# A fused attention and MLP kernel: the opening of token block 0 split by contraction chunk, gelu kept in PSUM, and block 1's input loaded later

## The chip, the cores and the metric

The kernel runs on one core of a Trainium2 chip. The metric is the device time of one execution in microseconds (us); lower is better. A measurement of this kernel is the median of several executions.

## The reference, cut to what matters

```python
xn = layernorm(x)                                  # x: 2048 tokens x 640
qkv = xn @ wqkv                                    # 32 heads of 20
phi(z) = concat(softmax(z @ w_phi[h]), softmax(-(z @ w_phi[h])))
A = (phi(q) @ (phi(k)^T v)) / (phi(q) @ sum(phi(k)) + 1e-6) @ wo
y = layernorm(xn)
B = gelu(y @ w1 + b1) @ w2 + b2                    # 640 -> 1728 -> 640
out = x + A + B
```

Everything is float32. The kernel splits each operand into a high and a low float32r part and makes a product of three matmuls (high times high, high times low, low times high).

## The kernel before, in words

The 2048 tokens are four blocks of 512. The results are kept transposed, as five chunks of 128 features by 512 tokens (`acc[b]`, which begins as the block's transposed x). The hidden layer of the MLP has 14 chunks of 128, taken two at a time (g = 0 to 6). For one pair and one block, a **pass** (`passes`) makes two hidden chunks, each of 15 matmuls of 128x512 with y as the right side (L70, L71 and L72, in `mm3`), then gelu on ScalarE (L286), a split of its result into `hh` and `hl` (copy on ScalarE at L61, subtraction on VectorE at L64), and then five output tiles of six matmuls each with the hidden pair as the right side. VectorE adds each output tile to `acc[b]` (L329 for g = 0, L331 later), and this frees the tile's PSUM bank. Output tiles take banks 5, 6, 7 in turn (`self.po`), so the fourth tile of a row of tiles waits until the first has been added. Hidden chunks take banks 0, 1, 2 (`self.ph`).

**The opening** is written out by hand: TensorE, VectorE, ScalarE and GpSimd run their instructions in the order of the code there. Block 0 is prepared from x itself. Four tiles of 128 tokens are loaded (`xb`); VectorE takes their means and variances (L138, L139); ScalarE subtracts the mean (L166, `centre`); each tile is multiplied by its factor `ry` (`scale`: even tiles on VectorE at L172, odd ones on ScalarE at L170); TensorE transposes the 128x128 pieces (L181, `make_y0`), and ScalarE and VectorE split the transposed pieces into the high and low part of `y[0]`. This is done for two tiles (256 tokens) at a time. After each half come 30 matmuls of 128x256 (L549, `half_first`): they make that half of the hidden chunks 0 and 1. Their results are turned into hidden values later by the list `zs`. Before the first transposes, 18 matmuls on zeros (L579) run.

**Block 1** is prepared otherwise: its means and factors are turned into rows by one small transpose (L197, `rows`), written to DRAM from ScalarE's DMA queue (L202), and read back as one broadcast of 128 x 1024 values (L207, `m<-r`). From `acc[1]` (all of x transposed, loaded at L512), GpSimd subtracts the row of means, chunk by chunk (L677); VectorE multiplies by the row of factors (L679), ScalarE makes the high part (L681) and VectorE the low part (L683). These steps are spread over the matmuls of block 0 by the generator `next_y`: one step of it runs at each `tick`, which is once for three matmuls.

DMAs of the main queue are issued by SyncE, in an order that a scheduler chooses; `issue_after` holds a DMA behind another in that order. The other lines that the text names: L63 copies weights on VectorE, L193 gathers the means for the rows, L199 takes the transposed rows out of PSUM, L646 multiplies attention weights, L669 subtracts in the attention weights `wpt`, L775 to L803 prepare blocks 2 and 3 in the same way later.

```python
p00 = mlp.passes(0, 0, [wc[0], wc[1]], hid)     # output tiles of block 0, hidden chunks 0 and 1
mlp.beside = next_y()
p10 = mlp.passes(1, 0, [wc[2], wc[3]])          # hidden chunks 2 and 3 of block 0
next(p10)                                       # its two hidden chunks
finish(p00)                                     # five output tiles
for m, _ in enumerate(p10): ...                 # five more
```

After these, block 1 begins with the hidden chunks 0 and 1.

Of the kernel before, what the change touches and what calls it, by code (L numbers as in the profile page):

```python
# [8 lines left out]
F32 = mybir.dt.float32  # L9
F32R = mybir.dt.float32r  # L10
AF = mybir.ActivationFunctionType
ALU = mybir.AluOpType
# [39 lines left out]
def tile_kernel(ctx: ExitStack, tc: tile.TileContext, x, xT, wkT, wqT, wv, wphi, wo, w1, b1, w2, b2,  # L52
                ident, mmask, emask, vsel, out):
    nc = tc.nc
# [43 lines left out]
    acc = [None] * NB  # L98
# [69 lines left out]
    def scale(t, xb, act=False):  # L168
        if act:
            nc.scalar.activation(xb, xb, AF.Copy, scale=ry[:, t:t + 1])  # L170
        else:
            nc.vector.tensor_scalar_mul(xb, xb, ry[:, t:t + 1])  # L172

    def make_y0(half, xbs, ptile):

        cols = slice(half * 256, half * 256 + 256)
        for c0, n in ((0, 2), (2, 2), (4, 1)):
            ps = ptile()
            for c in range(n):
                for i in range(2):  # L180
                    nc.tensor.transpose(ps[:, c * 256 + i * P:c * 256 + (i + 1) * P],  # L181
                                        xbs[i][:, (c0 + c) * P:(c0 + c + 1) * P], idt)
            src = ps[:, :n * 256].rearrange("p (c t) -> p c t", c=n)
            cs = slice(c0, c0 + n)
            split(y[0][0][:, cs, cols], y[0][1][:, cs, cols], src)
            yield

    def rows(b, n, xp, ptile, wait, queue=nc.sync):

        sc = xp.tile([P, n, 2, 4], F32, name="sc", bufs=1)  # L190
        ts = slice(4 * b, 4 * b + 4 * n)
        for a, src in enumerate((mv[:, ts, 0], ry[:, ts])):
            nc.vector.tensor_copy(sc[:, :, a, :], src.rearrange("p (b t) -> p b t", b=n))  # L193
        for _ in range(wait):
# [7 lines left out]
        queue.dma_start(r_dram[n].rearrange("b r t -> (b r) t"), sr)  # L202
# [8 lines left out]
    loads = {}  # L211


    class Mlp:
# [67 lines left out]
        def gelu(self, g, j, pz, gt, hh, hl, out=False):  # L282
            if out:
                nc.vector.tensor_copy(gt, pz)
                pz = gt
            nc.scalar.activation(gt, pz, AF.Gelu_apprx_tanh, bias=b1t[:, 2 * g + j:2 * g + j + 1])  # L286
            split(hh, hl, gt)

        def passes(self, g, b, ws, hid=None):


            yh, yl = y[b]
            self.turn ^= 1
            todo = ()
            if hid is None:
                hid, todo, gts = [], ws, mtile(4)
            for j, (w1h, w1l, w2h, w2l) in enumerate(todo):
                gt = gts[:, j, :512]
                hs = mtile(self.hid[self.turn][j], F32R)
                hh, hl = hs[:, 0, :512], hs[:, 1, :512]  # L300
                if not (g == 6 and j == 1):
                    self.first(g, j, b, ws[j], gt, hh, hl)
                    hid.append((hh, hl))
                else:
                    pz = self.ph()
                    for kc in range(KC):
                        nc.tensor.matmul(pz, w1h[:, kc, :], yh[:, kc, :], start=kc == 0, stop=False)
                        nc.tensor.matmul(pz, w1l[:, kc, :], yl[:, kc, :], start=False, stop=kc == KC - 1)
                    tm = gt[0:64, :]
                    nc.scalar.activation(tm, pz[64:128, :], AF.Copy)  # L310
                    nc.vector.tensor_tensor(tm, pz[0:64, :], tm, op=ALU.add)
                    nc.scalar.activation(gt[0:64, :], tm, AF.Gelu_apprx_tanh, bias=b1t[0:64, 13:14])
                    nc.scalar.activation(hh[0:64, :], gt[0:64, :], AF.Copy)
                    nc.gpsimd.tensor_tensor(hh[64:128, :], gt[0:64, :], f(hh[0:64, :]), op=ALU.subtract)
                    hid.append((hh, None))
            yield
            for m in range(KC):
                pw = self.po()
                ms = slice(m * P, (m + 1) * P)
                for j, (hh, hl) in enumerate(hid):  # L320
                    w2h, w2l = ws[j][2:]
                    if hl is not None:
                        mm3(pw, w2h[:, ms], w2l[:, ms], hh, hl, j == 0, j == 1)
                        self.tick()
                    else:
                        nc.tensor.matmul(pw, w2h[:, ms], hh, start=False, stop=False)  # L326
                        nc.tensor.matmul(pw, w2l[:, ms], hh, start=False, stop=True)  # L327
                if g == 0:
                    nc.vector.scalar_tensor_tensor(acc[b][:, m, :], pw, b2t[:, m:m + 1], acc[b][:, m, :], op0=ALU.add, op1=ALU.add)  # L329
                else:  # L330
                    nc.vector.tensor_tensor(acc[b][:, m, :], pw, acc[b][:, m, :], op=ALU.add)  # L331
                yield
# [178 lines left out]
    def load_acc(b):  # L511
        nc.sync.dma_start(acc[b], xT[:, b * 512:(b + 1) * 512].rearrange("(c p) t -> p c t", p=P))  # L512
# [4 lines left out]
    mlp = Mlp((0, 1, 2, 3), ((0, 2), (1, 3)))  # L517
# [19 lines left out]
    gts = mtile(4)  # L537
# [4 lines left out]
    def half_first(half, *order):  # L542

        cols = slice(half * 256, half * 256 + 256)
        pz = [pall()[:, cols] for _ in range(2)]
        last = {op[0]: op for op in order}
        for j, wi, yi in order:
            for kc in range(KC):
                nc.tensor.matmul(pz[j], wc[j][wi][:, kc, :], y[0][yi][:, kc, cols],  # L549
                                 start=(wi, yi, kc) == (0, 0, 0), stop=kc == KC - 1 and last[j] == (j, wi, yi))  # L550
        return [lambda j=j: mlp.gelu(0, j, pz[j], *[m[:, cols] for m in (gts[:, j, :512], *hid[j])]) for j in range(2)]

    x1 = load_x(range(4, 8), xp)
    for c, pool in ((2, None), (3, r0)):
# [27 lines left out]
    centre(0, x0[0])  # L582
    step(s01, 3)
    centre(1, x0[1])
    scale(0, x0[0])
    scale(1, x0[1], True)
    parts[0][0]()
    step(s23, 2)
    y01, y23 = make_y0(0, x0[:2], pall), make_y0(1, x0[2:], pall)
# [3 lines left out]
    step(s23, 1)  # L593
    centre(2, x0[2])
    centre(3, x0[3])
    scale(2, x0[2])
    scale(3, x0[3], True)
    zs = half_first(0, *((j, wi, yi) for j in range(2) for wi, yi in ((0, 0), (1 - j, j), (j, 1 - j))))
    parts[2][0]()
    step(s47, 2)  # L600
    step(y23, 4)
    zs += half_first(1, *((j, wi, yi) for ops in (((0, 0), (1, 0)), ((0, 1),)) for j in range(2) for wi, yi in ops))
    parts[3][0]()
    step(s47, 2)
    step(s01, 1)
    step(s47, 1)
    step(s47, 1)
    rows1 = rows(1, 1, xp, Banks(3), 1, nc.scalar)
    next(rows1)
    for c in range(2):  # L610
        parts[c][1](nc.vector)
# [41 lines left out]
    def next_y():  # L653

        for _ in range(3):
            yield
        next(rows1)
        for z in zs[:2]:
            z()
        finish(rows1)  # L660
        mr = load_rows(1)
        first_raws.extend(raws(jobs[0]))
        for z in zs[2:]:
            z()
        for c in range(2, 4):
            parts[c][1]()
        for _ in range(4):
            yield
        nc.vector.tensor_tensor(wpt[:, :, :, 1:], wpt[:, :, :, 1:], wpt[:, :, :, 0:1].to_broadcast([G6, 6, 6, DF]), op=ALU.subtract)  # L669
        for _ in range(9):  # L670
            yield
        xcs = {}
        for n in range(2 * KC + 5):
            c, i = divmod(n, 2)
            if i == 0 and c < KC:
                xcs[c] = xp.tile([P, D], F32, name="xb")[:, :512]
                nc.gpsimd.tensor_tensor(xcs[c], acc[1][:, c], mr[:, 0], op=ALU.subtract)  # L677
            if i == 0 and 0 <= (d := c - 1) < KC:
                nc.vector.tensor_tensor(xcs[d], xcs[d], mr[:, 1], op=ALU.mult)  # L679
            if i == 1 and 0 <= (d := c - 1) < KC:  # L680
                nc.scalar.activation(y[1][0][:, d], xcs[d], AF.Copy)  # L681
            if i == 0 and 0 <= (d := c - 2) < KC:
                nc.vector.tensor_tensor(y[1][1][:, d], xcs[d], f(y[1][0][:, d]), op=ALU.subtract)  # L683
            yield
        for st in (s23, s47):
            step(st, 1)
            yield
# [924 lines left out]
```

## Time and profile before

| | |
|---|---|
| median of 3 runs | 708.85 us (708.53 to 711.32) |
| the profiled execution | 709.98 us |
| its span, first to last instruction | 708.2 us |
| TensorE (PE) busy | 700.9 us, 99% of the span |
| VectorE (DVE) busy | 526.1 us, 74% |
| GpSimd (POOL) busy | 439.2 us, 62% |
| ScalarE (ACT) busy | 352.7 us, 50% |
| granted TensorE clock | 1.0 |

PEld is TensorE's loading of weights, which runs ahead of the matmuls. A row of the timeline has the start, the time taken, the engine, the line, the operation, what it writes and reads, the shape, how many instructions are merged in it, and in brackets the idle time of the engine before it and what ended that. A row of the waits has who waited for whom, the total in us, how often, and the longest. A row of the groups has the busy time and the mean in ns.

### The profile page before, as it was taken

How to read it: one execution, taken by the hardware profiler on the slowest of the kernel's cores; microseconds unless marked ns; L12 is line 12 of the kernel's file. 1: busy time of each engine (PE TensorE's matmuls, PEld its weight loads, DVE VectorE, ACT ScalarE, POOL GpSimd, SP SyncE). 2: the span in 40 equal slices, each digit the busy share in tenths (PEclk: the TensorE clock that was granted, in tenths of full speed). 3: DMA queues.
4: the chain of work that ended last, by engine and by line, in shares of the span. 5: the costliest groups of instructions: out<-in, count | busy, mean ns of one | idle time of the engine just before them, and what ended most of it. 6: DMA issues, size and time to landing. Idle time of an engine off the chain costs nothing.

```text
span 708.2 us, 9785 instructions
## 1 busy us (share of the span) xinstructions
PE 700.9 (99%) x3369; PEld 589.1 (83%) x3369; DVE 526.1 (74%) x840; ACT 352.7 (50%) x583; POOL 439.2 (62%) x374
## 2 busy tenths in 40 slices
PE   8999999999999999999999999999999999999998
PEld 7788888878888888888888888878888888888886
DVE  7877755978754788788888877838688686786773
ACT  6534554444433544554544546457676667561250
POOL 3621314567245998798787969558689997552530
PEclk9999999999999999999999999999999999999999
DMA  9823643475622227325500707874355659537212
GB/s 322 284 83 114 189 123 98 156 252 175 219 97 93 75 94 221 96 88 195 128 0 4 188 0 292 238 228 120 115 152 161 179 154 304 204 124 272 81 60 104
DMA packets 66296, 107.61 MB, mean 152 GB/s; under 512 B 7479, under 2 KB 31831, under 8 KB 64367
## 3 DMA queue, kind: packets, MB, share of 16 engines
q1 hardware_dynamic: 65942, 106.98, 47.5%
q8 instruction: 26, 0.43, 0.2%
q14 instruction: 24, 0.19, 0.1%
q10 hardware_dynamic: 304, 0.01, 0.0%
HBM read 72.42 MB, written 34.55 MB: 151 GB/s over the span
## 4 chain that ended last, share of the span: by engine, by line
PE 86%; DVE 5%; DMA 2%; issue 2%; POOL 2%; ACT 2%; SPq 1%; ACTq 0%; POOLq 0%; DVEq 0%
PE bank L906 28%; PE bank L70 16%; PE bank L71 16%; PE bank L72 16%; PE bank L976 3%; PE bank L646 2%; PE bank L1214 1%; PE bank L1215 1%; DMA t<-t 1%; DMA xb<-in_x 1%; DMA xq<-in_xT 1%; POOL w L64 1%; DVE st L138 1%; PE bank L327 1%; PE bank L326 1%
## 5 line engine op out<-in xcount | busy, mean ns | idle before, releaser
L906 PE MATMUL bank<-wkh,y 128*128 128x512 f32 (+1 forms) x480 | 139.5, 364 | 0.0
L64 POOL TENSOR_TENSOR w<-r,w 128x640 fp32r<-128x640 f32 x32 | 52.2, 1647 | 93.2 <-ACT w L61 63.4
L70 PE MATMUL bank<-m,w 128*128 128x512 f32 x274 | 108.1, 394 | 1.6 <-DVE acc L329 1.0
L71 PE MATMUL bank<-m,w 128*128 128x512 f32 x274 | 106.7, 389 | 0.0
L70 PE MATMUL bank<-y,w 128*128 128x512 f32 (+1 forms) x274 | 106.5, 389 | 0.0
L71 PE MATMUL bank<-y,w 128*128 128x512 f32 (+1 forms) x274 | 106.0, 387 | 0.0
L72 PE MATMUL bank<-y,w 128*128 128x512 f32 (+1 forms) x270 | 104.3, 386 | 0.0
L72 PE MATMUL bank<-m,w 128*128 128x512 f32 x262 | 102.0, 389 | 0.0
L906 PEld LDWEIGHTS bank<-wkh,y 128*128 128x128 f32 x480 | 87.5, 188 | 13.3
L906 PE MATMUL bank<-wkl,y 128*128 128x512 f32 (+1 forms) x240 | 87.4, 364 | 0.0
L942 ACT ACTIVATE m<-m,rs_all 128x1280 f32<-128x1280 f32 x32 | 43.7, 1365 | 42.9 <-POOL m L941 42.8
L70 PEld LDWEIGHTS bank<-m,w 128*128 128x128 f32 x274 | 51.5, 188 | 13.7 <-DVE acc L331 1.6
L70 PEld LDWEIGHTS bank<-y,w 128*128 128x128 f32 x274 | 51.5, 188 | 10.8 <-issue 0.4
L71 PEld LDWEIGHTS bank<-y,w 128*128 128x128 f32 x274 | 51.5, 188 | 10.5 <-DMA y<-t 0.3
L71 PEld LDWEIGHTS bank<-m,w 128*128 128x128 f32 x274 | 51.5, 188 | 10.2
L72 PEld LDWEIGHTS bank<-y,w 128*128 128x128 f32 x270 | 50.7, 188 | 10.3
L944 DVE TENSOR_REDUCE sm<-m 128x64 f32<-128x1280 f32 x32 | 47.4, 1482 | 15.0 <-ACT m L942 14.8
L72 PEld LDWEIGHTS bank<-m,w 128*128 128x128 f32 x262 | 49.2, 188 | 10.4
L906 PE MATMUL bank<-w,y 128*128 128x512 f32 x240 | 57.4, 391 | 0.0
L941 POOL TENSOR_TENSOR m<-m,mx 128x640 f32<-128x640 f32 (+2 forms) x48 | 44.4, 938 | 19.3 <-DVE mx L930 19.3
L331 DVE TENSOR_TENSOR acc<-bank,acc 128x512 f32<-128x512 f32 x70 | 46.9, 684 | 10.5 <-PE bank L72 5.3
L64 DVE TENSOR_TENSOR m<-m,m 128x512 fp32r<-128x512 f32 (+1 forms) x34 | 28.8, 854 | 34.4 <-ACT m L61 34.4
(216 smaller groups left out, 1517.2 us busy)
## 6 DMA issues: line engine op xcount, KB each, us to landing
r<-in_w SPq DMA_DIRECT2D x52, 320.0 KB
e<-e SPq DMA_DIRECT2D x40, 256.0 KB
e<-acc SPq DMA_DIRECT2D x52, 160.0 KB
acc<-in_xT SPq DMA_DIRECT2D x4, 1280.0 KB
t<-t SPq DMA_DIRECT2D x8, 512.0 KB
tf<-t SPq DMA_DIRECT2D x2, 1536.0 KB
xb<-in_x SPq DMA_DIRECT2D x8, 320.0 KB
t<-in_x SPq DMA_DIRECT2D x8, 320.0 KB
```

What stands on the lines that cost most here:

```text
L64: eng.tensor_tensor(lo, src, f(hi), op=ALU.subtract)
L70: nc.tensor.matmul(ps, lh, rh, start=first, stop=False, **kw)
L71: nc.tensor.matmul(ps, lh, rl, start=False, stop=False, **kw)
L72: nc.tensor.matmul(ps, ll, rh, start=False, stop=last, **kw)
L138: nc.vector.bn_stats(st[:, i, h, :], xb[:, h * 320:(h + 1) * 320])
L331: nc.vector.tensor_tensor(acc[b][:, m, :], pw, acc[b][:, m, :], op=ALU.add)
L646: nc.tensor.matmul(ps[:, u * nh * DF:(u + 1) * nh * DF], raw[:nh * DH, u * P:(u + 1) * P], wpt[:nh * DH, g, :nh, 1:], start=True, stop=True)
L906: nc.tensor.matmul(ps, lh[:, kc, c], rh[:, kc], start=n == 0, stop=n == 3 * KC - 1)
L941: subs[n, t] = nc.gpsimd.tensor_tensor(ep[:, s], a, b, op=ALU.subtract)
L942: exps[n, t] = nc.scalar.activation(e, e, AF.Exp, scale=rs_all[:, t:t + 1])
L944: nc.vector.tensor_reduce(sm, e.rearrange("p s (h f) -> p (s h) f", f=DH), axis=AX, op=ALU.add)
L976: nc.tensor.matmul(kvp[g // 2][:, (g % 2) * 240:(g % 2) * 240 + 240].rearrange("p (s f) -> p s f", s=4), v[:, g * VS:(g + 1) * VS], ft[:, ...
```

## The change

It has five parts.

1. In `make_y0` the transposed pieces come as one chunk, two chunks, two chunks (before: two, two, one). The odd tile of each pair is scaled in two pieces: the first 384 features on ScalarE and the last 256 on VectorE.
2. In the second half of block 0, the 20 matmuls that use the high part of y are ordered by contraction chunk (kc), over both hidden chunks and both parts of the weights. The ten with the low part follow. The first half keeps its order.
3. For blocks 0 and 1, gelu writes back into the PSUM bank that it reads, and the split reads that bank (before: an SBUF tile `gt`).
4. Block 1's `acc[1]` is not loaded with the early DMAs but behind `m<-r`, in two DMAs of two and three chunks. The row of means goes through a corner of `acc[1]`, and its transpose uses bank 7.
5. The row's DMA is issued after the first of the four half gelus instead of the second. The split of w2's chunk 2 has its copy on VectorE. The subtraction in `wpt` comes before the splits of the hidden chunks 2 and 3, and the split of w2's chunk 3 comes later.

```diff
+    def scale_pair(t):
+        scale(t, x0[t])
+        scale(t + 1, x0[t + 1][:, :3 * P], True)
+        scale(t + 1, x0[t + 1][:, 3 * P:])
     def make_y0(half, xbs, ptile):
-        for c0, n in ((0, 2), (2, 2), (4, 1)):
+        for c0, n in ((0, 1), (1, 2), (3, 2)):
     def rows(b, n, xp, ptile, wait, queue=nc.sync):
-        sr = xp.tile([8 * n, P], F32, name="sr16", bufs=1)
+        sr = acc[1][:8, 0, :P] if b == 1 else xp.tile([8 * n, P], F32, name="sr16", bufs=1)
     def gelu(self, g, j, pz, gt, hh, hl, out=False):
+            gt = pz if gt is None else gt
             nc.scalar.activation(gt, pz, AF.Gelu_apprx_tanh, bias=b1t[:, 2 * g + j:2 * g + j + 1])
             split(hh, hl, gt)
-                    self.first(g, j, b, ws[j], gt, hh, hl)
+                    self.first(g, j, b, ws[j], gt if b > 1 else None, hh, hl)
-    load_acc(1)
-    zs += half_first(1, *((j, wi, yi) for ops in (((0, 0), (1, 0)), ((0, 1),)) for j in range(2) for wi, yi in ops))
+    zs += half_first(1, *((j, wi, 0, kc) for kc in range(KC) for j in range(2) for wi in range(2)),
+                     *((j, 0, 1, kc) for j in range(2) for kc in range(KC)))
-    rows1 = rows(1, 1, xp, Banks(3), 1, nc.scalar)
+    rows1 = rows(1, 1, xp, Banks(7), 1, nc.scalar)
     def next_y():
         next(rows1)
-        for z in zs[:2]:
-            z()
+        zs[0]()
         finish(rows1)
         mr = load_rows(1)
+        with tc.issue_after(loads[1]):
+            for c0, c1 in ((0, 2), (2, KC)):
+                nc.sync.dma_start(acc[1][:, c0:c1], xT[c0 * P:c1 * P, 512:1024].rearrange("(c p) t -> p c t", p=P))
-        for z in zs[2:]:
+        for z in zs[1:]:
             z()
-        for c in range(2, 4):
-            parts[c][1]()
-        for _ in range(4):
-            yield
+        parts[2][1](nc.vector)
         nc.vector.tensor_tensor(wpt[:, :, :, 1:], wpt[:, :, :, 1:], wpt[:, :, :, 0:1].to_broadcast([G6, 6, 6, DF]), op=ALU.subtract)
-        for _ in range(9):
+        for _ in range(7):
+            yield
+        parts[3][1]()
+        for _ in range(6):
             yield
```

What stands on VectorE from the last half gelu of block 0 to the first additions to `acc[0]`, before (`m_149` and `m_389` are the SBUF tiles with the gelu, `m_390` and `m_438` the hidden chunks 2 and 3, `acc_103` is `acc[0]`):

```order
L64 TENSOR_TENSOR m_151<-m_149,m_151 128x256
L64 TENSOR_TENSOR m_390<-m_389,m_390 128x512
L669 TENSOR_TENSOR wpt<-wpt 120x36x19
L64 TENSOR_TENSOR m_438<-m_389,m_438 128x512
L329 SCALAR_TENSOR_TENSOR acc_103<-bank_459,b2t,acc_103 128x512
```

and after, on the same engine at the same place:

```order
L64 TENSOR_TENSOR m_150<-bank_325,m_150 128x256
L63 CAST w_172<-r_160 128x640
L670 TENSOR_TENSOR wpt<-wpt 120x36x19
L64 TENSOR_TENSOR m_390<-bank_391,m_390 128x512
L64 TENSOR_TENSOR m_438<-bank_439,m_438 128x512
L335 SCALAR_TENSOR_TENSOR acc_103<-bank_458,b2t,acc_103 128x512
```

The subtractions read PSUM banks, `wpt` stands ahead of both, and a copy of weights has come in.

What SyncE issues from the last early load to the first attention weights (`raw`), before (`acc_104` is `acc[1]`, `m_415` the broadcast rows of block 1):

```order
L512 DMA acc_104<-in_xT 128x5x512
L618 DMA wpt<-in_wphi 120x720
L207 DMA m_415<-r_84 128x1024
L637 DMA raw<-in_wkT 120x512
```

and after:

```order
L620 DMA wpt<-in_wphi 120x720
L212 DMA m_411<-r_84 128x1024
L665 DMA acc_104<-in_xT 128x2x512
L665 DMA acc_104<-in_xT 128x3x512
L639 DMA raw<-in_wkT 120x512
```

Block 1's transposed x now stands behind the rows, ahead of the attention weights.

More of the change, by code (lines that the diff above doesn't have):

```diff
@@ L546, in half_first @@
         last = {op[0]: op for op in order}
[L547 to L551, printed above, removed]
+        for op in order:
+            j, wi, yi, kc = op
+            nc.tensor.matmul(pz[j], wc[j][wi][:, kc, :], y[0][yi][:, kc, cols], start=(wi, yi, kc) == (0, 0, 0), stop=last[j] == op)
+        return [lambda j=j: mlp.gelu(0, j, pz[j], None, *[m[:, cols] for m in hid[j]]) for j in range(2)]
     x1 = load_x(range(4, 8), xp)
@@ L595, in tile_kernel @@
     centre(3, x0[3])
-    scale(2, x0[2])
-    scale(3, x0[3], True)
-    zs = half_first(0, *((j, wi, yi) for j in range(2) for wi, yi in ((0, 0), (1 - j, j), (j, 1 - j))))
+    scale_pair(2)
+    zs = half_first(0, *((j, wi, yi, kc) for j in range(2) for wi, yi in ((0, 0), (1 - j, j), (j, 1 - j)) for kc in range(KC)))
     parts[2][0]()
```

6 lines of the change are left out of this document (2 added, 4 removed).

## The prediction

> **What bounds the kernel now.** The page comes first: TensorE is busy for nearly all of the span, so an edit off its path is worth nothing, and a gain can only come from the places where it stands still. These are found in the waits of the weight loads (PEld), which show a late release more sharply than the overlapping matmuls do.
>
> ```profile
> PE 700.9 (99%) x3369; PEld 589.1 (83%) x3369; DVE 526.1 (74%) x840; ACT 352.7 (50%) x583; POOL 439.2 (62%) x374
> ```
>
> ```profile
> PEld bank L70 <- DVE acc L331: 1.6, 3, 0.7
> PEld bank L70 <- DVE acc L329: 1.4, 1, 1.4
> ...
> PEld bank L181 <- DVE xb L172: 1.1, 1, 1.1
> PEld bank L549 <- ACT y L61: 0.9, 4, 0.3
> ```
>
> Next the timeline of TensorE in the opening: the two runs of 30 half-width matmuls, the first full ones, the stall in block 0's output tiles, and the first matmul of block 1.
>
> ```profile
> 9.52 4.33 PE L549 MATMUL bank<-y,w 128*128 128x256 f32 x30
> ...
> 15.30 4.14 PE L549 MATMUL bank<-y,w 128*128 128x256 f32 x30
> 19.27 0.40 PE L70 MATMUL bank<-y,w 128*128 128x512 f32 x1
> ...
> 26.25 0.39 PE L70 MATMUL bank<-m,w 128*128 128x512 f32 x1
> ...
> 30.11 0.39 PE L72 MATMUL bank<-m,w 128*128 128x512 f32 x1
> 31.47 0.50 PE L70 MATMUL bank<-m,w 128*128 128x512 f32 x1 [0.97 <-DVE acc L329]
> ...
> 42.97 0.40 PE L70 MATMUL bank<-y,w 128*128 128x512 f32 x1
> ```
>
> Full matmuls start 0.23 us apart (30 of them from 19.27 to 26.25, the small transpose of the rows among them), so after 30.11 the next was due at 30.34: the stall is 1.13 us. The change reaches five places: the two halves of the opening, this stall, the start of block 1 at 42.97, and the three waits on L331, which lie in later passes of blocks 0 and 1.
>
> **Part 1 and 2: the opening.** The copies that make y's high part, the subtractions that make its low part, and the weight loads of the second half:
>
> ```profile
> L61 ACT ACTIVATE y<-bank x6: 391/592/598, 8.9 to 15.6; 128x512 fp32r<-128x512 f32 x4, 128x256 fp32r<-128x256 f32 x2
> ```
>
> ```profile
> 15.78 3.44 PEld L549 LDWEIGHTS bank<-y,w 128*128 128x128 f32 x28 [0.19 <-ACT y L61]
> ```
>
> ```profile
> 15.70 1.57 DVE L64 TENSOR_TENSOR y<-bank,y 128x512 fp32r<-128x512 f32 x3
> ```
>
> ```profile
> L172 DVE TENSOR_SCALAR xb<-xb,ry 128x640 f32<-128x640 f32 x2 | 1.1, 554 | 0.1
> ```
>
> A first copy of 256 instead of 512 columns ends 0.59 - 0.39 = 0.20 us sooner, so the matmuls can begin 0.2 us sooner in each half. In the first half this is not kept: its low-part matmuls stand in the middle and wait for VectorE, which now also scales 256 features more (less than the 0.55 of a whole tile) ahead of them. I take 0, between 0.2 gained and 0.2 lost. In the second half 20 matmuls now stand ahead of the low part. At 3.44 / 28 = 0.12 us each, 30 take 3.7 us without a break; they took 19.27 - 15.30 = 3.97. With 0.2 at the start and 0.27 in the middle this gives **0.5 us** (0 to 0.7). The low part ends at 15.70 + 1.57 = 17.27, and first use would be at 15.1 + 20 x 0.12 = 17.5: the cover is 0.2 us, and if VectorE is late by more, that comes off.
>
> **Part 3 and 5: the stall at 30.34.** The fourth output tile waits for the first addition to `acc[0]` (L329). What VectorE did before it, and the price of the same subtraction with and without a PSUM operand:
>
> ```profile
> 27.48 1.89 DVE L64 TENSOR_TENSOR m<-m,m 128x512 fp32r<-128x512 f32 x1 [1.62 <-ACT m L61]
> 29.29 0.86 DVE L669 TENSOR_TENSOR wpt<-wpt 120x684 f32<-120x684 f32 x1
> 30.07 0.68 DVE L64 TENSOR_TENSOR m<-m,m 128x512 fp32r<-128x512 f32 x1
> 30.67 2.06 DVE L329 SCALAR_TENSOR_TENSOR acc<-bank,b2t,acc 128x512 f32<-128x512 f32 x3
> 33.16 0.75 DVE L329 SCALAR_TENSOR_TENSOR acc<-bank,b2t,acc 128x512 f32<-128x512 f32 x1 [0.43 <-PE bank L72]
> ```
>
> ```profile
> 25.66 3.16 POOL L64 TENSOR_TENSOR w<-r,w 128x640 fp32r<-128x640 f32 x2 [0.75 <-ACT w L61]
> 31.42 7.66 POOL L677 TENSOR_TENSOR xb<-acc,m 128x512 f32<-128x512 f32 x5 [2.61 <-DMA m<-r]
> ```
>
> ```profile
> L331 DVE TENSOR_TENSOR acc<-bank,acc 128x512 f32<-128x512 f32 x70 | 46.9, 684 | 10.5 <-PE bank L72 5.3 <-PE bank L327 4.7
> ...
> L64 DVE TENSOR_TENSOR m<-m,m 128x256 fp32r<-128x256 f32 x4 | 3.3, 889 | 0.0
> ...
> L64 DVE TENSOR_TENSOR y<-bank,y 128x256 fp32r<-128x256 f32 x2 | 0.8, 417 | 0.0
> ```
>
> The subtraction at 27.48 took 1.89 us while GpSimd worked, and 0.68 at 30.07 when GpSimd was idle. The addition at 33.16 reads a bank; GpSimd worked beside it, and it took 0.75. So a subtraction that reads a bank is priced at 0.42 (256 columns) and 0.68 (512), GpSimd busy or not. The Trainium skill says the same on its page "SBUF — State Buffer", section "Who interferes with whom": VectorE with two SBUF inputs and GpSimd shut each other out for a whole instruction; the rows above agree (1.89 against 0.68). Against the change speaks its page "Perfetto Trace Analysis", section "Optimizing Scalar/DVE Operations", which puts VectorE's access at about 125 ns for PSUM and 60 for SBUF; by it, six subtractions would cost an estimated 0.4 us more, but L331 with its bank at 684 ns beside 0.68 for the SBUF form shows no such difference, so the sum goes by the rows.
>
> When VectorE gets to the first addition is now set by ScalarE:
>
> ```profile
> 22.64 0.53 ACTq L202 DMA_DIRECT2D r<-sr  x1
> ...
> 24.86 1.35 ACT L61 ACTIVATE w<-r 128x640 fp32r<-128x640 f32 x2
> ...
> 28.05 0.63 ACT L61 ACTIVATE m<-m 128x512 fp32r<-128x512 f32 x1
> ```
>
> Its copy of the second hidden chunk ended at 28.68. The weight copies ahead of it go (1.35; one to VectorE, one behind), the row's DMA now holds up three half gelus instead of two (at most 0.53 more), and VectorE's statistics, which feed the gelu, come some 0.2 later: about 28.1. Then a subtraction (0.68) and an addition (2.06 / 3 = 0.69) end near 29.5. `wpt` and the copy of weights fall into the wait before. TensorE would want the fourth tile at 30.34 - 0.5 = 29.84, so the stall goes: **1.13 us** (0 if ScalarE is 1.5 late). The PSUM banks are held some 2 us longer by a hidden chunk; bank 6 of the half gelus is next written by the second output tile at about 27.1 and is read last at about 26: covered by 1 us.
>
> **Part 4: block 1.** Before, its rows were the late item, not `acc[1]`:
>
> ```profile
> 12.96 0.38 SPq L512 DMA_DIRECT2D acc<-in_xT  x1
> ...
> 26.89 0.36 SPq L207 DMA_DIRECT2D m<-r  x1
> ```
>
> ```profile
> 16.00:24.00 8.00, 8.00 (x50) 7.06 (x50) 6.95 (x24) 4.56 (x10) 4.41 (x4) 1.00 1.05 377
> 24.00:31.00 7.00, 6.49 (x29) 5.05 (x27) 5.38 (x7) 4.59 (x9) 4.06 (x3) 1.00 0.55 152
> ```
>
> ```profile
> 44.35 0.68 DVE L683 TENSOR_TENSOR y<-xb,y 128x512 fp32r<-128x512 f32 x1
> ```
>
> The row's DMA was issued at 22.64 and `m<-r` could start at 26.89, 4.2 us later, with the queues full until 24 (377 GB/s). Without the 1280 KB of `acc[1]`, which take 1280 / 377 = 3.5 us, the queues are empty at about 21, and I put `m<-r` at 24.5 to 25. Then 512 + 1280 KB at 377 GB/s are in by 30. GpSimd is held by the last weight split until about 30.3 (copies of 1.35 / 2 from 28.1, then 3.16 / 2), so it starts at 30.3 instead of 31.42, 1.1 sooner. TensorE comes 0.5 + 1.13 = 1.63 sooner. Last low part before: 45.03; first use: 42.97 + 12 x 0.23 = 45.7. Of that slack of 0.7, 0.7 + 1.1 - 1.6 = 0.2 is left. I take 0 (0 to 0.5 lost).
>
> **Later passes.** The later passes of blocks 0 and 1 have more such subtractions. One stands ahead of an addition that TensorE waited for:
>
> ```profile
> 151.83 1.57 DVE L64 TENSOR_TENSOR m<-m,m 128x512 fp32r<-128x512 f32 x1 [0.55 <-ACT m L61]
> 153.33 0.68 DVE L331 TENSOR_TENSOR acc<-bank,acc 128x512 f32<-128x512 f32 x1
> ```
>
> ```profile
> 154.06 0.19 PEld L70 LDWEIGHTS bank<-m,w 128*128 128x128 f32 x1 [0.73 <-DVE acc L331]
> ```
>
> At 0.68 instead of 1.57 it ends 0.9 sooner, more than the 0.7 waited: that goes. Of the other 0.9 us of the three waits I take a third. Together **1.0 us** (0 to 1.5).
>
> **The sum.** 0.5 + 0 + 1.13 + 0 + 1.0 = 2.6 us. The profiled execution, 709.98 with 1.8 around its span, would become 707.4; the median of the runs, 708.85, is 1.1 below it, and from there the forecast is **706.3 us**. All stalls together give at most 0.9 + 1.13 + 1.5 = 3.5 us, 705.3.
>
> **The rivals.** *The wait moves.* If ScalarE is late (the DMA's hold and the later table of gelu add up) the first addition again ends near 31, and the early matmuls only wait longer. For it: both edits stand right ahead of the chain at 22.64. Against: 1.35 us of copies leave it. The 1.63 shrink to 0 to 0.6, the later 0.5 to 1.0 stay: 707.3 to 708.4, middle 707.9.
>
> *Block 1 comes late.* Slower: the loads behind `m<-r` move at 152 GB/s, as in 24 to 31 us, not at 377, and the row's DMA still waits until 26.89. Place: GpSimd's first subtraction and the third. The 1280 KB take 8.6 us behind rows that landed at 31.42: the third chunk would be there near 40, and the last low part some 6 us after that, near 46.5 to 48, against a wish of 44.1. The loss of 2.4 to 4 outweighs 1.6. It decides from a GpSimd start (or third chunk) 2.8 us later than I put it: with that the opening's gain is gone. Price: 0.8 to 2.4 slower before the later gain, 708.7 to 711.3, middle 709.7. Against it: the queues ran at 377 when full.
>
> *More than the waits show.* The reordering also mends small breaks under the matmuls' overlap: 704.5 to 705.3.
>
> **How the numbers follow.** Forecast 0.58 (705.3 to 707.3), the wait moves 0.2, block 1 late 0.14, more than shown 0.08. A change of 0.5%, 3.5 us, is about what a measurement of this kernel can tell from none. Below 705.3: 0.08 and the forecast's own edge, 0.05: 0.13. Above 712.4: only a late block 1 beyond its worst row, 0.05. Within: 0.82. The range leaves out the upper part of a late block 1 and half of the last case: 704.9 to 709.4.
>
> **What would show it.** Right: full matmuls begin near 18.8; no wait on the first addition near 29.8; subtractions `m<-bank,m` at 0.68 with GpSimd busy; `m<-r` issued by 25; block 1's first matmul near 41.3; the wait at 154 gone. Wrong: a wait of TensorE for y's low part in the second half or in block 1, GpSimd starting after 33, or a longer hold of PSUM banks as a wait on L64.

## The result, and the profile after

The median of the kernel after is 706.97 us (706.22 to 707.67, 8 runs), that of the kernel before, run beside it, 709.29 us (708.53 to 711.32, 8 runs): ratio 0.9964 with a 95% interval of 0.9953 to 0.9975, that is 1.8 to 3.3 us less. The forecast was 706.3 and its range 704.9 to 709.4. The profiled execution took 706.98 us, its span is 705.2 us at a granted clock of 1.0.

The page's first part. TensorE was at 99% before, too; its busy time went from 700.9 to 699.8, VectorE's from 526.1 to 519.1.

```profile
PE 699.8 (99%) x3369; PEld 589.8 (84%) x3369; DVE 519.1 (74%) x843; ACT 349.7 (50%) x582; POOL 439.4 (62%) x374
```

The waits of the weight loads in the kernel after, in total, times and longest. The wait of 1.4 us on the first addition to `acc[0]` (L329 before, L335 now) is not in the list any more, nor a wait of 0.7 us near 154; of those on the later additions of these passes one is left, at 191.7; a wait of 0.3 us near 615 is new. The second row is the wait for y's low part in the first half of the opening, at 11.7.

```profile
PEld bank L70 <- DVE acc L337: 0.7, 1, 0.7
...
PEld bank L554 <- DVE y L64: 0.3, 1, 0.3
```

The timeline of TensorE in the kernel after at the places that the prediction showed: both halves of the opening, the first full matmul, the first matmul of the fourth output tile, and the first of block 1.

```profile
9.09 4.92 PE L554 MATMUL bank<-y,w 128*128 128x256 f32 x30
...
14.86 3.88 PE L554 MATMUL bank<-y,w 128*128 128x256 f32 x30
18.58 0.40 PE L70 MATMUL bank<-y,w 128*128 128x512 f32 x1
...
29.64 0.39 PE L70 MATMUL bank<-m,w 128*128 128x512 f32 x1
...
41.00 0.40 PE L70 MATMUL bank<-y,w 128*128 128x512 f32 x1
```

Full matmuls start at 18.58 instead of 19.27. The fourth output tile starts at 29.64, without a wait, instead of 31.47; its matmul takes 0.39 us, where the one behind the stall took 0.50. What VectorE did ahead of that tile, and GpSimd beside it:

```profile
25.73 0.87 DVE L670 TENSOR_TENSOR wpt<-wpt 120x684 f32<-120x684 f32 x1
26.51 0.68 DVE L64 TENSOR_TENSOR m<-bank,m 128x512 fp32r<-128x512 f32 x1
27.36 0.69 DVE L64 TENSOR_TENSOR m<-bank,m 128x512 fp32r<-128x512 f32 x1 [0.17 <-ACT m L61]
27.97 1.40 DVE L335 SCALAR_TENSOR_TENSOR acc<-bank,b2t,acc 128x512 f32<-128x512 f32 x2
```

```profile
25.90 3.71 POOL L64 TENSOR_TENSOR w<-r,w 128x640 fp32r<-128x640 f32 x2 [1.14 <-DVE w L63]
29.79 7.64 POOL L681 TENSOR_TENSOR xb<-acc,m 128x512 f32<-128x512 f32 x5 [0.18 <-DMA acc<-in_xT]
```

Both subtractions lie inside GpSimd's splits and take 0.68 and 0.69 us; before, the first took 1.89 beside GpSimd. GpSimd's splits are what got longer (3.71 for the two instead of 3.16): the first starts under `wpt`'s subtraction and takes 2.14 us, against 1.58 in the run below where that subtraction comes later. Nobody waits for it. The subtraction in `wpt` itself stays at 0.87, because it comes first: GpSimd's split waits for the copy of weights on VectorE (L63), which part 5 has put right ahead of `wpt`, and so begins 0.17 us behind it (25.90 after 25.73).

Laying the k-th weight load of the one trace beside the k-th of the other gives the lead of after over before: 0.69 us at the first full matmul, 1.97 after the first output tiles, still 1.95 at 149, 2.55 behind 154, 2.61 behind 194, 3.11 behind 470 and 2.93 at the end. The first two steps are the edits at work. Against a second execution of the kernel before, shown further down, the lead is 2.0 us from there to 190 and 1.6 at the end, so the rest is not there each time.

### The profile page after: what moved, and what is told of

The parts are those of the page before. It is cut to its first block, busy times and chain, and to the rows that moved or that the text cites. A ratio compares the mean times of both kernels' runs of the same rounds, so it can differ in the third digit from the quotient of the medians.

```text
span 705.2 us, 9792 instructions
## 1 busy us (share of the span) xinstructions
PE 699.8 (99%) x3369; PEld 589.8 (84%) x3369; DVE 519.1 (74%) x843; ACT 349.7 (50%) x582; POOL 439.4 (62%) x374
## 4 chain that ended last, share of the span: by engine, by line
PE 89%; DVE 4%; DMA 3%; issue 1%; POOL 1%; ACT 1%; SPq 0%; POOLq 0%; ACTq 0%; DVEq 0%
PE bank L910 28%; PE bank L70 17%; PE bank L72 16%; PE bank L71 16%; PE bank L980 3%; PE bank L648 2%; DMA t<-t 2%; PE bank L1218 1%; PE bank L1219 1%; PE bank L554 1%; DMA xq<-in_xT 1%; POOL w L64 1%; PE bank L332 1%; PE bank L333 1%; PE bank L1150 1%
## 5 line engine op out<-in xcount | busy, mean ns | idle before, releaser
L1212 POOL TENSOR_TENSOR e<-e,m 128x512 fp32r<-128x512 f32 x28 | 41.7, 1493 | 15.9 <-ACT m L1211 13.1
```

Source lines behind the costliest of these rows:

```text
L1212: mlp.after(1, lambda: nc.gpsimd.tensor_tensor(pl, e, f(ph), op=ALU.subtract))
```

## The experiments

In every run below the same comparison of weight loads is used. "The stall" is the wait of the weight loads ahead of the fourth output tile, 1.36 us in the kernel before (1.40 in the list, less the 0.04 us that lie between any two full loads; other waits are counted in the same way).

### Which edit removes the stall

**The gelu in PSUM alone.** The kernel before with part 3; the rows' transpose takes bank 7, as it does after.

```
-        self.first(g, j, b, ws[j], gt, hh, hl)
+        self.first(g, j, b, ws[j], gt if b > 1 else None, hh, hl)
-        ... m for m in (gts[:, j, :512], *hid[j])
+        None, *[m[:, cols] for m in hid[j]]
-    rows1 = rows(1, 1, xp, Banks(3), 1, nc.scalar)
+    rows1 = rows(1, 1, xp, Banks(7), 1, nc.scalar)
```

> The kernel before with part 3 alone (gelu in the PSUM bank for blocks 0 and 1; the rows' transpose in bank 7, since bank 3 now holds a hidden chunk). Theory (the subtraction with two SBUF inputs was held by GpSimd): the subtraction at 27.48 takes 0.68 instead of 1.89, the first addition ends near 30.3, the fourth output tile starts near 30.5 instead of 31.47, block 1 near 42.1 instead of 42.97, and the wait at 154 is gone: the span is 1.5 to 2 us shorter, ratio to before 0.9973. Rival (ScalarE's chain and the order of the steps set the first addition): the fourth tile still starts after 31.2, and only the wait at 154 goes, 0.6 us.

Measured: 708.01 us against 709.81, ratio 0.9978 (0.9967 to 0.9989). Its waits and VectorE's timeline:

```profile
PEld bank L70 <- DVE acc L330: 0.6, 1, 0.6
```

```profile
27.20 0.69 DVE L64 TENSOR_TENSOR m<-bank,m 128x512 fp32r<-128x512 f32 x1 [2.01 <-ACT m L61]
27.80 1.45 DVE L669 TENSOR_TENSOR wpt<-wpt 120x684 f32<-120x684 f32 x1
29.18 0.68 DVE L64 TENSOR_TENSOR m<-bank,m 128x512 fp32r<-128x512 f32 x1
```

The subtraction is short beside GpSimd (whose splits run from 25.43 to 28.53), but the next instruction, `wpt`'s subtraction with both operands in SBUF, inherits the hold: 1.45 instead of 0.86. The fourth tile starts at 30.57 and the wait near 154 is gone, as expected. Part 3 alone leaves 0.6 of the stall.

**The gelu in SBUF.** The kernel after without part 3: the two lines of the gelu above, the other way round.

> The changed kernel with gelu in the SBUF tile again (part 3 undone). Theory: the subtractions stand beside GpSimd's weight splits from 25.9 to 29.6 and take 0.9 to 1.9 us; the first addition ends near 30.3 to 31 instead of 28.7, the fourth tile starts 0.7 to 1.3 later than its 29.64, and a wait comes back near 152: the span is 1.3 to 2 us longer than the changed kernel's 705.2. Rival (the new order of the steps alone clears the stall): the fourth tile stays within 0.2 us of 29.64 and only the wait near 152 comes back, 0.6 us.

Measured: 708.21 us, ratio 0.9980 (0.9968 to 0.9992). The stall is back, and two SBUF subtractions together take 2.29 us:

```profile
PEld bank L70 <- DVE acc L335: 0.9, 1, 0.9
```

```profile
8.52 0.89 DVE L138 BATCH_NORM_STATS2 st<-xb 128x6 f32<-128x320 f32 x2 [0.49 <-DMA xb<-in_x]
...
27.75 2.29 DVE L64 TENSOR_TENSOR m<-m,m 128x512 fp32r<-128x512 f32 x2 [0.30 <-ACT m L61]
```

Two things did not come as expected. No wait came back near 152, and the opening lost 0.5 of its gain, because a tile of x landed 0.5 us late (the first row). Both are taken up below.

**The gelu in PSUM in the opening only.** The kernel after; the half-width chunks stay in PSUM, the full-width ones of the passes go to SBUF.

```
-        self.first(g, j, b, ws[j], gt if b > 1 else None, hh, hl)
+        self.first(g, j, b, ws[j], gt, hh, hl)
```

> The kernel after with its gelu kept in PSUM in the opening alone; the passes of blocks 0 and 1 after it write it to an SBUF tile as before. If the prediction's step is right, a wait of 0.4 to 0.7 us comes near 152, and the time is 707.4 to 707.8. Rival (the opening's length decides who begins first there): TensorE has no wait over 0.2 us between 140 and 160, and the time is within 0.3 us of the kernel after, 706.7 to 707.3.

Measured: 708.69 us against 709.64, ratio 0.9988 (0.9980 to 0.9997). Near 152 nothing over 0.2 us, as the rival said, but neither had foreseen the stall at the fourth tile:

```profile
PEld bank L70 <- DVE acc L335: 1.9, 1, 1.9
```

```profile
26.53 4.04 DVE L64 TENSOR_TENSOR m<-m,m 128x512 fp32r<-128x512 f32 x2
```

```profile
25.92 4.11 POOL L64 TENSOR_TENSOR w<-r,w 128x640 fp32r<-128x640 f32 x2 [1.15 <-DVE w L63]
```

With ScalarE and `wpt` out of the way sooner, each of the two subtractions starts under one of GpSimd's two splits and takes 2.06 us. So with the operand in SBUF part 5 gains hardly anything here: the fourth tile starts at 31.29, against 31.47 in the kernel before. TensorE was ready for it 0.7 us sooner, which is why the wait is longer (1.9). In the run above only one of the subtractions met a split, and the wait was 0.9.

**The gelu in PSUM in the passes only.** The kernel before with the line of the passes alone; this is the complement.

```
+            gt = pz if gt is None else gt
-        self.first(g, j, b, ws[j], gt, hh, hl)
+        self.first(g, j, b, ws[j], gt if b > 1 else None, hh, hl)
```

> The kernel before with one thing of part 3 alone: the gelu is kept in PSUM in the passes of blocks 0 and 1 after the opening; the opening keeps its SBUF tile. If the prediction's step is right (the subtraction there, 0.68 us instead of 1.57 beside GpSimd, is what removed the wait of 0.7 us near 154), TensorE runs level with the kernel before until 150, and the wait near 154 is gone: lead 0 before it and 0.5 to 0.7 after it, 708.9 or less against 709.6. Rival (that wait hangs on whether GpSimd or VectorE begins first there, which the opening's length shifts): the wait near 154 stays at 0.5 to 0.7, lead 0 to 0.1 there, and the time within 0.3 us of the kernel before.

Measured: 709.12 us, ratio 0.9991 (0.9981 to 1.0000). The expectation of no lead before 150 was mistaken: the chunks ahead of the first output tiles come from that line too, so the stall went to 0.75 us and the lead to 0.61. Near 154 the wait is gone:

```profile
151.31 0.69 DVE L64 TENSOR_TENSOR m<-bank,m 128x512 fp32r<-128x512 f32 x1 [0.49 <-ACT m L61]
```

```profile
150.97 1.29 POOL L776 TENSOR_TENSOR xq<-xq,m 128x512 f32<-128x512 f32 x1 [2.03 <-DMA xq<-in_xT]
```

GpSimd began 0.34 us ahead of the subtraction, as it did in the kernel before (0.26), and the subtraction still took 0.69 instead of 1.57.

**The old steps.** The kernel after without part 5.

```
-        zs[0]()
+        for z in zs[:2]:
+            z()
-        parts[2][1](nc.vector)
+        for c in range(2, 4):
+            parts[c][1]()
+        for _ in range(4):
+            yield
         nc.vector.tensor_tensor(wpt[:, :, :, 1:], ...
...
```

> The kernel after without part 5: both first gelu steps before the rows' copy, the weight splits of parts 2 and 3 together with ScalarE doing the copy, the subtraction on wpt four steps later. Theory (the stall at the fourth output tile went in two halves: shorter subtractions in PSUM, and the wpt subtraction standing ahead of GpSimd's long split): the first full matmul stays near 18.6, but the wpt subtraction meets GpSimd's split again and lasts about 1.4 us instead of 0.87, so the fourth output tile waits 0.4 to 0.9 us and begins at 30.0 to 30.6 instead of 29.64; the rest as in the kernel after, in all 707.3 to 707.9. Rival (the subtractions in PSUM alone removed the stall): no wait over 0.2 at the fourth output tile, 706.9 to 707.1.

Measured: 708.45 us, ratio 0.9980 (0.9972 to 0.9989). The stall is 1.0 us (1.1 in the list), and `wpt`'s subtraction took 1.46 again. The fourth tile began at 31.32, later than either theory had it, since x was late in this execution by 0.75 us:

```profile
PEld bank L70 <- DVE acc L335: 1.1, 1, 1.1
```

```profile
8.91 0.89 DVE L138 BATCH_NORM_STATS2 st<-xb 128x6 f32<-128x320 f32 x2 [0.75 <-DMA xb<-in_x]
...
28.54 1.46 DVE L674 TENSOR_TENSOR wpt<-wpt 120x684 f32<-120x684 f32 x1
```

So it takes both edits to remove the stall. Its length, which also counts how early TensorE gets there, with the passes' subtractions in SBUF or PSUM and with the old or new steps:

| | old steps | new steps |
|---|---|---|
| full-width subtractions in SBUF | 1.4 | 0.9 and 1.9 |
| in PSUM | 0.6, 0.8 and 1.0 | none |

### Block 1's loads

The kernel after with `acc[1]` loaded ahead of everything again, as before.

```
     load_acc(0)
     for c in range(2, 4):
         dmas[c][1]()
+    load_acc(1)
...
-        with tc.issue_after(loads[1]):
-            for c0, c1 in ((0, 2), (2, KC)):
-                nc.sync.dma_start(acc[1][:, c0:c1], ...
```

> The changed kernel with block 1's transposed x loaded early in one DMA, as before (part 4 undone; the row of means has its own tile again). Theory: the row's DMA lands behind 1280 KB more, so the broadcast is issued near 26 instead of 23.24, GpSimd starts at 30.5 to 31 instead of 29.79, and the last low part of block 1 ends near 44.3 instead of 43.39, while TensorE wants it at 41.0 + 12 x 0.23 = 43.7: a new wait of 0.5 to 0.9 us near 43.7, and the span is as much longer. Rival (the early load was not in the way, the slack of VectorE covers it): no wait near 43.7, the span within 0.2 us of 705.2.

Measured: 708.55 us, ratio 0.9989 (0.9976 to 1.0001). The rows came as expected (issued at 26.08, GpSimd from 30.47). The wait expected at block 1 did not come, but TensorE was then 4.2 us later than in the kernel after, so this execution does not test it. A larger loss came earlier, at the fourth output tile, where the lead over the kernel before went from 0.8 to -2.3 us. VectorE's and TensorE's timelines, and the granted clock (the column behind GpSimd's):

```profile
28.14 2.10 DVE L668 TENSOR_TENSOR wpt<-wpt 120x684 f32<-120x684 f32 x1 [2.41 <-DMA wpt<-in_wphi]
```

```profile
32.15 0.50 PE L70 MATMUL bank<-m,w 128*128 128x512 f32 x1 [2.44 <-DVE acc L335]
```

```profile
32.10:33.60 1.50, 1.45 (x6) 1.24 (x7) 1.31 (x2) 0.00 (x0) 1.50 (x2) 1.00 1.03 391
33.60:37.40 3.80, 3.80 (x11) 2.94 (x10) 3.18 (x4) 0.63 (x1) 3.56 (x3) 0.55 0.99 377
```

Behind 1280 KB of `acc[1]`, `wpt` arrives later, and VectorE stands 2.4 us in front of its subtraction, which part 5 has put ahead of the hidden chunks. The subtraction then starts under a split of GpSimd (27.94 to 29.50) and takes 2.10 us instead of 0.87. The first addition waits behind both. TensorE stood for 2.4 us (the wait of its weight loads is 2.9), worked 1.5 us at a clock of 1.00, and then ran at 0.55 from 33.6 to 37.4. So parts 4 and 5 hang together: the early subtraction is only cheap because part 4 empties the queue ahead of `wpt`. This execution was the slowest of its ten timed ones (710.6 against a median of 708.55), so the other nine need not have stood for as long; what they lost, no trace shows.

### The opening

**The old opening.** The kernel after without parts 1 and 2.

```
-        for c0, n in ((0, 1), (1, 2), (3, 2)):
+        for c0, n in ((0, 2), (2, 2), (4, 1)):
-    scale_pair(0)
+    scale(0, x0[0])
+    scale(1, x0[1], True)
-    zs += half_first(1, *((j, wi, 0, kc) for kc in range(KC) for j in range(2) for wi in range(2)), ...
+    zs += half_first(1, ... the products one after the other, each over all chunks)
```

> The changed kernel with the transposes two, two, one, the odd tile scaled whole on ScalarE, and the second half by part of the weights (parts 1 and 2 undone). Theory: the first full matmul starts at 19.2 to 19.3 instead of 18.58, no new wait behind it, block 1 near 41.7 instead of 41.0, and the span is 0.6 to 0.7 longer. Rival (a lead in the opening is given back at the next wait, since VectorE's chain is the same): block 1 within 0.2 us of 41.0 and the span within 0.2 of 705.2.

Measured: 707.62 us, ratio 0.9963 (0.9949 to 0.9977). From the first transpose to the first full matmul it needs 11.23 us, the kernel before 11.21, the kernel after 10.53: the opening's 0.7 is there in the trace. Block 1 begins at 41.58 instead of 41.00, so TensorE keeps most of it until there. The medians, 707.62 and 706.97, differ by as much, but the kernel before moved by 0.5 between the two measurements (709.81 and 709.29), so the timed runs do not settle it.

**Without part 1 alone, and without part 2 alone** (the halves of the edit above):

> The kernel after without part 1 alone: token tiles scaled whole, transposes in groups of two, two and one chunk; the order of the second half's products by chunk stays. By the prediction's step (0.2 us of the opening's gain from the earlier start of the transposes, 0.27 from the products in the middle): 10.7 to 10.8 us from the first transpose to the first full matmul, instead of 10.53 with both and 11.22 with neither. Rival (the two only work together: without the smaller first group the order by chunk still waits for the copies): 11.0 to 11.2.

> The kernel after without part 2 alone: the second half's products in the old order, all chunks of one product before the next; transposes and scaling stay as in the kernel after. By the prediction's step: 10.8 to 10.9 us from the first transpose to the first full matmul. Rival (the transposes carry all of it, since the first group of one chunk lets TensorE begin and the copies keep ahead of it): 10.5 to 10.6.

In the first of these x was late again (0.71 us), which shifts the first half and its sum, 11.29 us. The sum of the second is 11.13, above both of its expectations. They took 707.28 and 707.29 us, in one execution each. The second half can be read by itself. The rows of the weight loads in the second half: kernel before, after, without part 1, without part 2; each from the first transpose to the first full load.

```profile
13.86 1.16 PEld L181 LDWEIGHTS bank<-idt,xb 128*128 128x128 f32 x10 [0.22 <-issue]
...
19.15 0.19 PEld L70 LDWEIGHTS bank<-y,w 128*128 128x128 f32 x1
```

```profile
13.75 1.12 PEld L186 LDWEIGHTS bank<-idt,xb 128*128 128x128 f32 x10
14.84 3.70 PEld L554 LDWEIGHTS bank<-y,w 128*128 128x128 f32 x30
18.46 0.19 PEld L70 LDWEIGHTS bank<-y,w 128*128 128x128 f32 x1
```

```profile
14.20 1.12 PEld L185 LDWEIGHTS bank<-idt,xb 128*128 128x128 f32 x10
15.68 3.65 PEld L553 LDWEIGHTS bank<-y,w 128*128 128x128 f32 x30 [0.36 <-ACT y L61]
19.26 0.19 PEld L70 LDWEIGHTS bank<-y,w 128*128 128x128 f32 x1
```

```profile
13.65 1.12 PEld L186 LDWEIGHTS bank<-idt,xb 128*128 128x128 f32 x10
14.74 0.19 PEld L554 LDWEIGHTS bank<-y,w 128*128 128x128 f32 x1
15.26 0.30 PEld L554 LDWEIGHTS bank<-y,w 128*128 128x128 f32 x2 [0.33 <-ACT y L61]
15.75 3.29 PEld L554 LDWEIGHTS bank<-y,w 128*128 128x128 f32 x27 [0.19 <-ACT y L61]
18.97 0.19 PEld L70 LDWEIGHTS bank<-y,w 128*128 128x128 f32 x1
```

5.29, 4.71, 5.06 and 5.32 us. Part 1 without part 2 gains nothing: the first product can start at 14.74, but asks for chunk 1 at once and waits 0.33 and 0.19 for its copy. Part 2 without part 1 gains 0.23: no break in the middle, but the start still waits 0.36 for the copy of two chunks. Together they gain 0.58. Neither theory fits alone; the edits work on two waits that lie one behind the other.

**A later low part in the first half, too.** The kernel after with this order, an attempt at the wait of 0.3 us that is left at 11.7:

```
-    zs = half_first(0, *((j, wi, yi, kc) for j in range(2) for wi, yi in ((0, 0), (1 - j, j), (j, 1 - j)) ...
+    zs = half_first(0, *((j, wi, yi, kc) for j, wi, yi in
+             ((0,0,0), (0,1,0), (1,0,0), (0,0,1), (1,0,1), (1,1,0)) for kc in range(KC)))
```

> The kernel after with another order of the opening's first half: the products of the high parts come first for both hidden tiles, those with y's low part after them, and only then the last product with the second tile's low weights. The wait of 0.30 us for y's low part near 11.7 goes, so TensorE begins the second half's transposes and with them the first full matmul 0.2 to 0.4 us sooner, near 18.3: 706.6 to 706.8. Rival (the start of the second half is set by y's own parts from VectorE and ScalarE, not by TensorE): the first full matmul stays at 18.5 to 18.6 and the time at 707.0.

Measured: 706.92 us (706.27 to 707.17) against 709.64, ratio 0.9960 (0.9948 to 0.9973). Its weight loads:

```profile
10.01 3.30 PEld L554 LDWEIGHTS bank<-y,w 128*128 128x128 f32 x27 [0.19 <-ACT y L61]
13.58 1.07 PEld L186 LDWEIGHTS bank<-idt,xb 128*128 128x128 f32 x10 [0.27 <-PE bank L554]
...
18.23 0.19 PEld L70 LDWEIGHTS bank<-y,w 128*128 128x128 f32 x1
```

The wait at 11.7 is gone, 27 loads follow each other; TensorE now stands 0.27 us ahead of the second transposes instead. From the first transpose (7.87) to the first full load it is 10.36 us, 10.53 in the kernel after: 0.2 us stay of the 0.2 to 0.4 expected. The ratio cannot be told from that of the kernel after.

### What belongs to the execution

Both kernels in one more profiled execution each, unchanged.

> The kernel before in one more profiled execution, to tell which of its waits belong to the code and which to the execution. Theory: the stall at the fourth output tile (1.36 us), the wait at 154 (0.7) and those at 65.5, 581 and 639 come again within 0.15 us, and only the opening moves by up to 0.5 us with the arrival of x; if so, the 0.5 us of waits near 465 to 470, absent from the kernel after and from three of the experiments, come again too and belong to the change. Rival (they belong to the execution, as the wait near 194 does, which ranged from 0 to 0.96 us over the runs so far): the waits at 154, 194 and 465 to 470 differ from the first profile by 0.3 us or more.

> The kernel after in one more profiled execution. Theory: no wait over 0.2 us at the fourth output tile nor near 152, since the subtractions there read PSUM and do not depend on when GpSimd begins; 10.5 us from the first transpose to the first full matmul; the wait near 192 may be anything from 0 to 1 us. Rival (the stall and the wait near 152 were avoided by the phase of that execution): either comes back with 0.3 us or more.

They took 708.62 and 707.66 us. The stall came again in the kernel before (1.36, as the first time) and was absent again in the kernel after, so that is the code. The waits at 65.5, 581 and 639 came again, too. The waits near 154, 169 and 465 to 470 did not. The one near 194 differed by only 0.12 us (0.45 after 0.57 in the list), less than the rival asked. In the kernel after the opening took 10.95 us instead of the expected 10.5: x was 0.29 late. Near 154, GpSimd in the first execution of before, then VectorE and GpSimd in the second:

```profile
151.57 1.29 POOL L775 TENSOR_TENSOR xq<-xq,m 128x512 f32<-128x512 f32 x1 [1.58 <-DMA xq<-in_xT]
```

```profile
151.19 0.69 DVE L64 TENSOR_TENSOR m<-m,m 128x512 fp32r<-128x512 f32 x1 [0.55 <-ACT m L61]
```

```profile
151.97 1.29 POOL L775 TENSOR_TENSOR xq<-xq,m 128x512 f32<-128x512 f32 x1 [1.88 <-DVE m L64]
```

The operand is in SBUF as in the first execution, but now the subtraction came ahead of GpSimd, took 0.69 instead of 1.57, and TensorE did not wait. In the first execution GpSimd, released by a transfer of `xq`, had come 0.26 us ahead. In the second the same transfer landed at 151.84, just ahead of GpSimd's start; the subtraction that the row names ended in the same instant, and the first execution shows that GpSimd need not wait for it. VectorE was also 0.64 us sooner. ScalarE shows why, in the first and in the second execution:

```profile
149.93 0.63 ACT L782 ACTIVATE t<-xq 128x512 fp32r<-128x512 f32 x1 [2.26 <-DMA t<-t]
```

```profile
149.08 0.63 ACT L782 ACTIVATE t<-xq 128x512 fp32r<-128x512 f32 x1 [1.32 <-DMA t<-t]
```

The gelu of the pass stands behind this instruction, which waits for another transfer; that came 0.85 us later in the first execution. So two transfers set the order there. The waits of the second execution of the kernel after show that waits can also appear: 1.0 us near 462 to 468, which its first execution had not, and which the kernel before had in its first (0.65) and not in its second.

```profile
PEld bank L70 <- ACT m L455: 0.8, 1, 0.8
...
PEld bank L71 <- DMA y<-t: 0.3, 1, 0.3
```

## Why the prediction was right

The time was right to 0.7 us, the sum of 2.6 us against 2.3 in the medians. In part this is luck: the first two gains came out 0.34 us larger than forecast (1.97 for 1.63), and the third, 1.0, is not borne out by the runs.

**Opening, first half: 0.** Held. The half began 0.4 sooner (9.09 after 9.52). It gave half of that back at once, waiting for the next copies (0.30 and 0.19 us), and then 0.4 at y's low part in its middle, which was forecast. Ahead of the second transposes, where the kernel before stands 0.22, it got 0.3 back; they began 0.1 sooner (13.75 against 13.86).

**Opening, second half: 0.5.** Measured 0.58, 0.69 in all. The two pieces of the step were sized 0.2 and 0.27; alone they are worth 0 and 0.23. The working added them as if they were independent; that they gave the right sum is because the one removes the wait that the other would run into. The working also says that 20 matmuls "now" stand ahead of the low part; in the kernel before it was 20, too, and what broke the row was the wait for the next copy (0.19 at 15.78). The cover of 0.2 us for the low part held: 30 loads in a row without a break.

**The stall: 1.13.** Measured 1.28. The stall went whole, at 29.64 against a wish of 29.84. Of the missing 0.15, 0.10 is that the matmul behind the wait takes longer (0.50 instead of 0.39, the next one starts 0.33 behind it instead of 0.23), which the step did not count; the rest is spread over the matmuls that follow. ScalarE was the late engine as said, but ended its second hidden copy at 27.33 instead of 28.1. The price of a subtraction that reads a bank, 0.68 from the rows of additions, measured 0.68 and 0.69. The Trainium skill's page "SBUF — State Buffer", section "Who interferes with whom", says that issue order decides who blocks; the runs agree, 0.69 us ahead of GpSimd and 1.57 behind it for the same SBUF operands, and 0.69 either way with a PSUM operand. Its page "Perfetto Trace Analysis" had spoken of a dearer access to PSUM; the subtractions of 512 columns here take 0.68 to 0.69 with either operand, as long as GpSimd does not hold them.

**Block 1: 0.** Held, with more slack than the 0.2 worked out. Here are the transfer of the rows and the last low part in the kernel after:

```profile
23.24 0.36 SPq L212 DMA_DIRECT2D m<-r  x1
```

```profile
42.71 0.68 DVE L687 TENSOR_TENSOR y<-xb,y 128x512 fp32r<-128x512 f32 x1
```

It was issued at 23.24 (forecast 24.5 to 25), GpSimd began at 29.79 (30.3), and the last low part ended at 43.39, 0.4 ahead of its first use, 41.00 + 12 x 0.23 = 43.8.

**Later passes: 1.0.** This is the step that the runs do not bear out. Its mechanism exists: with GpSimd 0.09 us ahead in the kernel after (the rows below) and 0.34 in the run with the passes alone in PSUM, the subtraction stays at 0.69. But the wait of 0.7 that it was to remove stood in only one of two executions of the kernel before, and was absent in both runs that kept the operand in SBUF, where VectorE began first, by 0.77 and 0.10 us. The step took it whole from one profile, and a third of the other waits with it, without asking how often they occur.

```profile
149.96 0.69 DVE L64 TENSOR_TENSOR m<-bank,m 128x512 fp32r<-128x512 f32 x1 [0.49 <-ACT m L61]
```

```profile
149.87 1.29 POOL L779 TENSOR_TENSOR xq<-xq,m 128x512 f32<-128x512 f32 x1 [2.28 <-DMA xq<-in_xT]
```

The part that comes again is 0.69 + 1.28 = 2.0 us. What is left of the medians is 0.3, or 0.7 to 0.8 against the 709.64 and 709.81 that the kernel before took beside the experiments; the interval of 1.8 to 3.3 us holds 2.0 as well as 2.6. A wait of 0.7 in a part of the executions would give something of this size. How large a part stays open: of those 59 runs of the kernel before only seven were as short as the second execution (708.62), so the waits that it lacks may well be there in most. The waits near 194, between 0 and 0.96 us over the runs, and near 470 differ between executions of the same kernel.

**The rivals.** ScalarE was not late, and the rows did not wait. The neighbour of "block 1 comes late" did show up when `acc[1]` was put back: a late load, but with `wpt` as the one that VectorE stands behind. Nothing beyond the waits was gained: 706.97 lies above the 705.3 of the third rival.

## What to carry to other kernels

Before a wait in a profile is put into a sum, ask whether what releases it hangs on a transfer's arrival; such a wait is worth its share of executions, and a second profile of the unchanged kernel shows it for the price of one run. An operand moved out of SBUF takes the instruction out of the race with GpSimd, but the next instruction with two SBUF operands inherits the hold, so look at the pair. An order that is meant to win that race is safe when GpSimd waits for something that stands just ahead on VectorE, as `wpt`'s subtraction does here. An instruction moved forward in a queue needs its data forward, too.

## What the runs showed of the hardware that was not expected

After a stand of 2.4 us (the kernel with `acc[1]` loaded early) TensorE first worked 1.5 us at full pace; then matmuls started 0.427 us apart instead of 0.228 for some 3.4 us, and the granted clock was 0.55 over the stretch. A stand of 1.5 us (the gelu in PSUM in the opening only) was not followed by it. The Trainium skill's page "TensorE: Matmul & The Clock Gate", section "Part 1: The HAM clock gate (the "warmup" mystery)", puts the slow clock behind an idle window of about 3.4 us; here the stand was shorter than that, and the drop came only when work had gone on for 1.5 us.

A VectorE instruction with two SBUF operands that GpSimd held up ended a fixed time after GpSimd's instruction: the 512-column subtraction 0.54 to 0.56 us (29.37 after 28.81 in the kernel before, 30.57 after 30.02 with the gelu in PSUM in the opening only), `wpt`'s 0.72 to 0.73 (29.25 after 28.53 with part 3 alone). So its length, 1.57 us in one place and 2.06 in another, is told by when GpSimd ends. The starts in the profile do not always tell who is held: at 544.33 in the kernel before, such a subtraction began 0.37 us behind GpSimd and still took 0.68.

A tile of x that the opening waits for kept VectorE waiting 0.20 to 0.75 us in five of the fourteen profiled executions, before's and after's code alike. A gain of 0.7 us there shows in a trace, measured within one half, and hardly in a run's time.
